# One visit of the array for the logits of two token groups, and one exponential for both, in a list-scheduled attention and gMLP kernel

## The chip, the cores and the metric

The kernel runs on one core of a Trainium2 chip. The metric is the device time of one execution in microseconds (us), as a median over runs. The engines are named as in the profile: PE (TensorE, matmuls), PEld (its weight loads), DVE (VectorE), ACT (ScalarE), POOL (GpSimd) and SP (SyncE, which here only issues transfers).

## The reference

Two branches share one normalised input and are added to it. Branch A is a local attention with 32 heads of 16: each token sees itself and seven earlier tokens, two apart. Branch B is a gated MLP whose gate is mixed over the tokens by a 2048 x 2048 matrix.

```python
xn = _layernorm(x)                                  # x: 2048 tokens x 512
# A
q, k, v = heads(xn @ wqkv)                          # 32 heads of 16
idx = pos[:, None] - 2 * arange(8)[None, :]         # masked where idx < 0
logits = einsum('bhsd,bhswd->bhsw', q, k[idx]) * 16 ** -0.5
A = einsum('bhsw,bhswd->bhsd', softmax(logits), v[idx]).reshape(B, S, D) @ wo
# B
z = _gelu(xn @ w_in); z1 = z[..., :896]; z2 = _layernorm(z[..., 896:])
g = einsum('ts,bsf->btf', w_sp, z2) + b_sp[None, :, None]
B = (z1 * g) @ w_out
out = x + A + B
```

## The kernel before, in words

The 2048 tokens are cut into 16 blocks of 128 and into 4 groups j of 512 (NJ = 4). Every step is recorded as a task with an engine, its inputs and outputs, a guessed duration and a priority. Then one list schedule (`Plan.schedule`, L123, called at L1004) walks through guessed time, picks for each engine the task that can start first (among those within `tol` ns of it, the one with the lowest priority number, L191), and gives each task that needs PSUM one of the 8 banks, or a pair of them. What comes out is a fixed order for each engine. On the chip each engine works through its order and waits on semaphores. The guessed rates and durations (`dma_bw`, `dma_lat`, `tol`, `est`) therefore change nothing but the orders and the choice of banks.

Steps that matter here, in rough order of time:

- Normalisation and transposes of x (to about 30 us); V of each block, `v_block` (L645), matmuls on L654, eviction by ACT on L663, a POOL-issued store to DRAM on L668 (tasks Vw0 to Vw15).
- `z2_block` (L752): the gate's input half, matmuls on L759, gelu and square on ACT (L767, L772). Four blocks at a time are normalised: small DVE steps L778 to L785, a power on POOL (L788, tasks zr0 to zr3), and four DVE scalings (L791).
- `qk_pair` (L671): Q and K of a group, matmuls on L677, one ACT eviction L686.
- `prods` (L690): for a group, four DVE products q*k over all 8 offsets (L698) and three DVE additions (L703), all 128x4096 in bf16. The sum lies in buffer `pb` 0 or 2 (`acc`, by the parity of j); buffer 1 holds the product that is to be added. Then PE sums over the four partitions that hold parts of one head: eight matmuls with a weight of only 32 columns (E32), each writing 32 of the 128 partitions of PSUM (L711, task red0 to red3). This is one **visit**; its result takes a pair of banks.
- `softmax` (L718): DVE takes the maximum out of PSUM (L726) and subtracts it, PSUM to SBUF (L728; smax and ssub), ACT computes exp in place on 128x1024 bf16 (L732, sexp), DVE sums, inverts and scales (L735 to L745), and SP issues a transpose of the weights (L747, attnT).
- `z1_group` (L798): the other half of the MLP, matmuls on L805, gelu on ACT (L811). exp and gelu come from different tables of ACT, so each change between them is a table load (shown as ACT_TABLE_LOAD).
- `g_group` (L883): the token mixing, 448 matmuls on L894, copied out by ACT (L902) and combined by DVE (L905, L908).
- `pv_block` (L911): per block, SP loads 8 shifted copies of V (L917, 1 MB each), DVE multiplies and adds (L922, L925, L928), SP transposes the result (L931).
- `out_block` (L936): both output projections into one bank (L950, L959), a DVE addition of x (L965), a store (L970).

SP has a single queue for nearly all transfers, and its order is part of the schedule too. Before the change, each group goes through `softmax(j, prods(j))` by itself (L851 to L854).

Of the kernel before, what the change touches and what calls it, by code (L numbers as in the profile page):

```python
# [11 lines left out]
ACTF = mybir.ActivationFunctionType  # L12
# [326 lines left out]
def build_kernel(nc, A_x, A_wqkv, A_wo, B_x, B_w_in, B_w_sp, B_b_sp, B_w_out, out, report=False, emit=True):  # L339
    S = A_x.shape[1]  # L340
    D = A_x.shape[2]
    assert D == 512 and S % 512 == 0
    NB = S // 128
    NJ = S // 512
# [14 lines left out]
    off = {}  # L359
# [34 lines left out]
    plan = Plan()  # L394

    with ExitStack() as es:
        ar = es.enter_context(nc.sbuf_tensor("arena", [128, AR], BF))
        fp = es.enter_context(nc.sbuf_tensor("fpool", [128, FR], F32))
        ps = es.enter_context(nc.psum_tensor("ps", [128, PR], F32))
        sem_h = {e: es.enter_context(nc.semaphore("sem_" + e)) for e in ENGS if e != "sp"}  # L400

        def A(name, n, o2_=0):
            return ar[:, off[name] + o2_: off[name] + o2_ + n]

        def AC(o_, dims):
            return bass.AP(tensor=ar, offset=o_, ap=[[AR, 128]] + [list(d) for d in dims])
# [73 lines left out]
        def c_act(n, psum=True, accum=False):  # L480
            return (170.0 if psum else 205.0) + n * 0.833 + (200.0 if accum else 0.0)
# [7 lines left out]
        T = plan.add  # L489

        def dma(eng, fn, nbytes, chan, reads=(), writes=(), name="", xbar=False, prio=0.0, after=()):
# [4 lines left out]
        E32 = A("E32", 32)  # L496
# [10 lines left out]
          writes=["ident"], est=300, name="ident1")  # L507
# [27 lines left out]
        def ld_wqk(which, eng):  # L535
# [6 lines left out]
            writes=[("xin0", 0), ("xin0", 1)], name="ldx0")  # L542
# [15 lines left out]
        for wi in range(NWARM):  # L558
            n_ = 512 if wi < 6 else 128
            T("pe", (lambda bw, n_: lambda t: t.matmul(P(bw, n_), ones[:, 0:128], ones[:, 0:n_], start=True,  # L560
                                                       stop=True))(bw, n_),
              writes=[bw], est=(427.0 if n_ == 512 else 107.0), name="warm%d" % wi, prio=1000)

        T("act", lambda a: a.activation(Fv("prime", 4), mhalf, ACTF.Gelu_apprx_tanh), reads=["mhalf"],
          writes=["prime"], est=1500, name="actprime", tbl="gelu")
# [105 lines left out]
        def qk_pair(j, c):  # L671
            bk = plan.bank("QK%d_%d" % (j, c), 2)
            for which in range(2):
                def mm(t, which=which):
                    last = None
                    for dc in range(4):
                        last = t.matmul(P(bk, 512, 512 * which),  # L677
                                        AC(off["wqk"] + 2048 * which + 512 * dc + c, [[4, 128]]),
                                        AC(off["xnT"] + dc * S + 512 * j, [[1, 512]]), start=(dc == 0),
                                        stop=(dc == 3))  # L680
                    return last
                T("pe", mm, reads=[("wqk", which)] + [("xnT", b) for b in range(4 * j, 4 * j + 4)], writes=[bk],
                  est=4 * c_mm(512), name="%s%d_%d" % ("QK"[which], j, c), prio=10 + 18 * j + c)
            qo = off["QT"] + 2048 * (j % 2) + 512 * c
            ko = off["KT"] + c * (S + KP) + KP + 512 * j
            T("act", lambda a: a.activation(AC(qo, [[ko - qo, 2], [1, 512]]),  # L686
                                            P(bk, 1024).rearrange("p (t n) -> p t n", t=2), ACTF.Copy, scale=0.5),
              reads=[bk], writes=[("QT", c, j % 2), ("KT", c, j)], est=c_act(1024), name="QKe%d_%d" % (j, c), prio=1)

        def prods(j):  # L690
            acc = (0, 2)[j % 2]
            for c in range(4):
                s_ = acc if c == 0 else 1
                qb = AC(off["QT"] + 2048 * (j % 2) + 512 * c, [[0, 8], [1, 512]])
                kb = AC(off["KT"] + c * (S + KP) + KP + 512 * j, [[-2, 8], [1, 512]])
                pbv = A("pb", 4096, 4096 * s_).rearrange("p (w s) -> p w s", w=8)
                rd = [("QT", c, j % 2), ("KT", c, j), ("KT", c, j - 1) if j > 0 else ("KTpad", c)]
                T("dve", (lambda pbv, qb, kb: lambda v: v.tensor_tensor(pbv, qb, kb, ALU.mult))(pbv, qb, kb),  # L698
                  reads=rd, writes=[("pb", s_)], est=c_tt(4096), name="prod%d_%d" % (j, c), prio=5 + j)
                if c > 0:  # L700
                    av = A("pb", 4096, 4096 * acc)
                    bv = A("pb", 4096, 4096 * 1)
                    T("dve", (lambda av, bv: lambda v: v.tensor_tensor(av, av, bv, ALU.add))(av, bv),  # L703
                      reads=[("pb", 1)], writes=[("pb", acc)], est=c_tt(4096), name="padd%d_%d" % (j, c), prio=5 + j)
            bk = plan.bank("lg%d" % j, 2)

            def mm(t):
                last = None
                for hf in range(2):
                    for a in range(4):  # L710
                        last = t.matmul(ps[32 * a:32 * a + 32, bk.col(512 * hf):bk.col(512 * hf) + 512], E32,  # L711
                                        AC(off["pb"] + 4096 * acc + 2048 * hf + 128 * a, [[512, 4], [1, 128]]),
                                        start=True, stop=True)
                return last
            T("pe", mm, reads=[("pb", acc), "E32"], writes=[bk], est=600.0, name="red%d" % j, prio=1)
            return bk

        def softmax(j, bk):  # L718
            ds = j % 2
            if j == 0:  # L720
                def msk(v):
                    lg = bass.AP(tensor=ps, offset=bk.col(), ap=[[PR, 32], [128, 8], [1, 16]])
                    return v.tensor_tensor(lg, lg, bass.AP(tensor=fp, offset=foff["maskt"],
                                                           ap=[[FR, 32], [16, 8], [1, 16]]), ALU.add)
                T("dve", msk, reads=["maskt"], writes=[bk], est=300, name="smask", prio=4)
            T("dve", lambda v: v.tensor_reduce(Fv("mx", 128), PC(bk.col(), [[1, 128], [128, 8]]), AX.X, ALU.max),  # L726
              reads=[bk], writes=["mx"], est=1218, name="smax%d" % j, prio=4)
            T("dve", lambda v: v.tensor_tensor(A("D", 1024, 1024 * ds).rearrange("p (w t) -> p w t", w=8),  # L728
                                               PC(bk.col(), [[128, 8], [1, 128]]),
                                               FCa(foff["mx"], [[0, 8], [1, 128]]), ALU.subtract),  # L730
              reads=[bk, "mx"], writes=[("D", ds)], est=1222, name="ssub%d" % j, prio=4)
            T("act", lambda a: a.activation(A("D", 1024, 1024 * ds), A("D", 1024, 1024 * ds), ACTF.Exp),  # L732
              writes=[("D", ds)], est=c_act(1024, psum=False), name="sexp%d" % j, tbl="exp", prio=(2, 7, 2, 2)[j], late=3)
            do = off["D"] + 1024 * ds
            T("dve", lambda v: v.tensor_tensor(A("Za", 512), A("D", 512, 1024 * ds), A("D", 512, 1024 * ds + 512),  # L735
                                               ALU.add),
              reads=[("D", ds)], writes=["Za"], est=c_tt(512), name="sz1_%d" % j, prio=4)
            T("dve", lambda v: v.tensor_tensor(Fv("Zb", 256), A("Za", 256), A("Za", 256, 256), ALU.add),
              reads=["Za"], writes=["Zb"], est=423, name="sz2_%d" % j, prio=4)
            T("dve", lambda v: v.tensor_tensor(Fv("Z", 128), Fv("Zb", 128), Fv("Zb", 128, 128), ALU.add),  # L740
              reads=["Zb"], writes=["Z"], est=292, name="sz3_%d" % j, prio=4)
            T("dve", lambda v: v.reciprocal(A("R", 128), Fv("Z", 128)), reads=["Z"], writes=["R"], est=952,
              name="srec%d" % j, prio=4)
            dv = A("D", 1024, 1024 * ds).rearrange("p (w t) -> p w t", w=8)
            T("dve", lambda v: v.tensor_tensor(dv, dv, AC(off["R"], [[0, 8], [1, 128]]), ALU.mult),  # L745
              reads=["R"], writes=[("D", ds)], est=c_tt(1024), name="sattn%d" % j, prio=4)
            dma("sp", lambda e: e.dma_start_transpose(AC(off["attn"] + 1024 * j, [[128, 8], [1, 128]]),  # L747
                                                      A("D", 1024, 1024 * ds)),
                128 * 1024 * 2, ("attnT", ds), reads=[("D", ds)], writes=[("attn", b) for b in range(4 * j, 4 * j + 4)],
                name="attnT%d" % j, xbar=True, prio=1)  # L750
# [66 lines left out]
        for b in range(8, NB):  # L817
# [10 lines left out]
          writes=[("KTpad", c) for c in range(4)], est=170, name="ktpad", prio=2, after=lnr[:8])  # L828
# [19 lines left out]
            512 * 896 * 2, "w_in1", writes=["w_in1"], name="ldwin1", prio=2, after=lnd[4:8])  # L848
        for j in range(NJ):
            z2_wave(j)  # L850
        for j in range(NJ):  # L851
            for c in range(4):
                qk_pair(j, c)
            softmax(j, prods(j))  # L854
        for j in range(NJ):
            for pr in PAIRS:
                z1_group(pr, j)
# [132 lines left out]
        for names in (["warm%d" % wi for wi in range(NWARM)] +  # L990
# [9 lines left out]
            for n0, n1 in zip(names, names[1:]):  # L1000
                if byname[n0] not in byname[n1].deps:
                    byname[n1].odeps.add(byname[n0])

        plan.schedule(tol=30.0, dma_bw=270.0, dma_lat=1300.0, overlap=40.0,  # L1004
                      land=dict(ldx0=3580.0, ldx1=4700.0, ldwv0=4050.0, ldwv1=5300.0, ldx2=5700.0, ldwin2a=6950.0, ldwin2b=8250.0,
                                ldx3=8650.0, ldx4=9050.0, ldx5=9400.0, ldx6=9750.0, ldx7=10200.0, ldq=11700.0, ldk=13200.0))
        if report:
# [49 lines left out]
```

## Time and profile before

| | |
|---|---|
| median of 3 runs | 238.06 us (237.9 to 238.14) |
| the profiled execution | 237.62 us |
| its span, first to last instruction | 236.2 us |
| granted TensorE clock | 1.000 |
| PE: matmuls | 1135 |
| matmuls of the token mixing (L894) | 97.0 us of PE's busy time |
| visits for the logits (L711) | 4, at 48.62, 71.62, 94.72 and 122.14 us |
| ACT: exp (L732) | 4 of 1055 ns, with 3 table loads |
| DVE: products and additions (L698, L703) | 28 of about 2.28 us |

The span is the time between the first and the last instruction of the program; the 1.4 us between it and the execution's time lie around the program. A matmul's busy time counts from its start to its modelled end, and the next one starts before that end. So the distance between the starts of two matmuls is what one of them costs, and not its duration. "x8" in a timeline stands for eight instructions of one kind that were merged into one row: the row has the start of the first and the time to the end of the last.

### The profile page before, as it was taken

To read this page: it belongs to the slowest core of one execution; us is meant where nothing else is said; L and a number is where in the kernel's file an instruction comes from. 1 tells how busy PE (TensorE), PEld (TensorE's weight loads), DVE (VectorE), ACT (ScalarE), POOL (GpSimd) and SP (SyncE) were. 2 spreads that over 40 slices of the span, in tenths; PEclk is the share of its full clock that TensorE was granted. 3 is DMA by queue.
4 is the path that set the end of the run, shared out by engine and by line. 5 is a ranking of instruction groups with operands and counts; after the bars stand their busy time and mean duration, and the time that the engine had idled before them with its cause. 6 is when DMAs were issued, how large, how long until landed. Compare 5 with 4: busy or idle time off the path is not lost.

```text
span 236.2 us, 2999 instructions
## 1 busy us (share of the span) xinstructions
PE 233.4 (99%) x1135; PEld 109.2 (46%) x1135; DVE 206.9 (88%) x269; ACT 98.8 (42%) x149; POOL 37.0 (16%) x56
## 2 busy tenths in 40 slices
PE   8999999999999999999999999999999999999996
PEld 3555555545444444444444444444444444444443
DVE  4799899999899999998899999844899998999732
ACT  3698989888979896631120311111111111000000
POOL 2268650312943400000000000000000000000000
DMA  6997969991058800430579999999666959944442
GB/s 205 362 286 192 205 152 218 172 217 42 3 191 284 166 31 20 148 77 10 193 241 322 214 217 253 242 230 326 205 207 206 276 176 248 290 131 156 111 134 69
DMA packets 82013, 43.86 MB, mean 186 GB/s; under 512 B 54336, under 2 KB 81360, under 8 KB 82000
## 3 DMA queue, kind: packets, MB, share of 16 engines
q1 hardware_dynamic: 80768, 41.27, 69.1%
q0 software_dynamic: 800, 2.11, 2.7%
q10 hardware_dynamic: 432, 0.30, 0.4%
q8 instruction: 9, 0.15, 0.2%
q14 instruction: 4, 0.03, 0.1%
HBM read 26.35 MB, written 4.21 MB: 129 GB/s over the span
## 4 chain that ended last, share of the span: by engine, by line
PE 99%; DVE 0%; issue 0%; DVEq 0%
PE ps L894 41%; PE ps L677 12%; PE ps L759 10%; PE ps L805 10%; PE ps L959 10%; PE ps L654 6%; PE ps L950 6%; PE ps L560 1%; PE ps L711 1%; PE ps L579 1%; PE ps L638 1%; DVE arena L965 0%; DVEq L319 0%
## 5 line engine op out<-in xcount | busy, mean ns | idle before, releaser
L894 PE MATMUL ps<-arena 128*128 128x512 bf16 x448 | 97.0, 379 | 0.0
L894 PEld LDWEIGHTS ps<-arena 128*128 128x128 bf16 x448 | 43.8, 98 | 53.0 <-issue 0.4
L902 ACT ACTIVATE arena<-ps 128x1024 bf16<-128x1024 f32 (+1 forms) x16 | 14.7, 917 | 78.8 <-PE ps L894 78.8
L922 DVE TENSOR_TENSOR arena<-arena 128x4096 bf16<-128x4096 bf16 x16 | 36.5, 2284 | 0.0
L698 DVE TENSOR_TENSOR arena<-arena 128x4096 bf16<-128x4096 bf16 x16 | 36.3, 2275 | 0.0
L925 DVE TENSOR_TENSOR arena<-arena 128x2048 bf16<-128x2048 bf16 (+1 forms) x32 | 30.3, 950 | 0.1
L677 PE MATMUL ps<-arena 128*128 128x512 bf16 x128 | 28.9, 379 | 0.0
L703 DVE TENSOR_TENSOR arena<-arena 128x4096 bf16<-128x4096 bf16 x12 | 27.4, 2282 | 0.0
L959 PE MATMUL ps<-arena 128*128 128x512 bf16 (+2 forms) x119 | 27.0, 366 | 0.0
L759 PE MATMUL ps<-arena 128*128 128x448 bf16 x128 | 26.0, 353 | 0.0
L805 PE MATMUL ps<-arena 128*128 128x512 bf16 x112 | 24.5, 379 | 0.0
L677 PEld LDWEIGHTS ps<-arena 128*128 128x128 bf16 x128 | 14.5, 114 | 13.0
L905 DVE TENSOR_TENSOR arena<-arena 128x1024 bf16<-128x1024 bf16 (+1 forms) x16 | 10.0, 623 | 11.2 <-ACT arena L902 11.1
L965 DVE TENSOR_TENSOR arena<-ps,arena 128x512 bf16<-128x512 f32 (+2 forms) x17 | 11.2, 657 | 9.0 <-PE ps L959 8.8
L759 PEld LDWEIGHTS ps<-arena 128*128 128x128 bf16 x128 | 12.4, 98 | 11.9 <-issue 0.4
L686 ACT ACTIVATE arena<-ps 128x1024 bf16<-128x1024 f32 x16 | 16.3, 1018 | 3.4 <-PE ps L677 2.2
L959 PEld LDWEIGHTS ps<-arena 128*128 128x128 bf16 x119 | 11.4, 98 | 12.8
L788 POOL TENSOR_TENSOR fpool<-fpool 128x4 f32<-128x4 f32 x4 | 14.3, 3583 | 18.0 <-DVE fpool L785 18.0
L805 PEld LDWEIGHTS ps<-arena 128*128 128x128 bf16 x112 | 10.9, 98 | 13.4 <-issue 0.4
L950 PE MATMUL ps<-arena 128*128 128x512 bf16 (+2 forms) x68 | 16.6, 366 | 0.0
L654 PE MATMUL ps<-arena 128*128 128x512 bf16 x64 | 16.6, 387 | 0.0
L811 ACT ACTIVATE arena<-ps 128x1024 bf16<-128x1024 f32 (+1 forms) x16 | 14.0, 920 | 5.3 <-PE ps L805 5.3
(62 smaller groups left out, 181.8 us busy)
## 6 DMA issues: line engine op xcount, KB each, us to landing
arena<-vscr SPq DMA_DIRECT2D x16, 1024.0 KB, 5.8
arena<-in_A_x_dram SPq DMA_DIRECT2D x30, 128.0 KB, 4.0
vscr<-arena POOLq DMA_DIRECT2D x16, 128.0 KB, 3.1
out_dram<-arena SPq DMA_DIRECT2D x15, 128.0 KB, 1.9
arena<-in_A_wqkv_dram SPq DMA_DIRECT2D x2, 512.0 KB, 6.1
arena<-in_B_w_in_dram SPq DMA_DIRECT2D x2, 448.0 KB, 5.4
arena<-in_B_w_in_dram SPq DMA_DIRECT2D x1, 896.0 KB, 5.6
arena<-in_B_w_out_dram SPq DMA_DIRECT2D x1, 896.0 KB, 5.3
```

Of the source, the lines that this page charges most:

```text
L654: last = t.matmul(P(bk, 512), A("xcT", 128, 512 * b + 128 * dc) if b < 2 else xTv(b, dc), A("wv", 512, 512 * dc), start=(dc == 0), stop=(d ...
L677: last = t.matmul(P(bk, 512, 512 * which), AC(off["wqk"] + 2048 * which + 512 * dc + c, [[4, 128]]), AC(off["xnT"] + dc * S + 512 * j, [[1 ...
L686: T("act", lambda a: a.activation(AC(qo, [[ko - qo, 2], [1, 512]]), P(bk, 1024).rearrange("p (t n) -> p t n", t=2), ACTF.Copy, scale=0.5), ...
L698: T("dve", (lambda pbv, qb, kb: lambda v: v.tensor_tensor(pbv, qb, kb, ALU.mult))(pbv, qb, kb), reads=rd, writes=[("pb", s_)], est=c_tt(40 ...
L703: T("dve", (lambda av, bv: lambda v: v.tensor_tensor(av, av, bv, ALU.add))(av, bv), reads=[("pb", 1)], writes=[("pb", acc)], est=c_tt(4096 ...
L759: last = t.matmul(P(bk, 448, 512 * hf), xTv(b, dc), AC(off["w_in2"] + 896 * dc + 448 * hf, [[1, 448]]), start=(dc == 0), stop=(dc == 3))
L805: last = t.matmul(P(bk, 512, 512 * i), AC(off["w_in1"] + 896 * dc + 128 * fc, [[1, 128]]), AC(off["xnT"] + dc * S + 512 * j, [[1, 512]]), ...
L894: last = t.matmul(P(bk, 512, 512 * i), AC(off["z2"] + FH * sh + 128 * fc, [[1, 128]]), AC(off["wT%d" % r_] + sh * 512, [[1, 512]]), start= ...
L922: T("dve", lambda v: v.tensor_tensor(tv, tv, av, ALU.mult), reads=[("attn", b)], writes=[("Vs", sv)], est=c_tt(4096), name="pv%d" % b, pri ...
L925: T("dve", (lambda n: lambda v: v.tensor_tensor(A("Vs", n, 4096 * sv), A("Vs", n, 4096 * sv), A("Vs", n, 4096 * sv + n), ALU.add))(n), wri ...
L950: last = t.matmul(P(bk, cn), AC(off["OT"] + 512 * tb + 128 * cc, [[1, 128]]), AC(off["wo"] + 512 * cc + c0, [[1, cn]]), start=(cc == 0), s ...
L959: last = t.matmul(P(bk, cn), AC(off["z1T"] + fc * S + 128 * tb, [[1, 128]]), AC(off["w_out"] + 512 * fc + c0, [[1, cn]]), start=False, sto ...
```

## The change

The matmuls of two groups' logits become one task, which waits for both groups' sums and writes two pairs of banks. The maximum and the subtraction stay one per group, and one exponential over 128x2048 then does both groups. The loop takes the groups in pairs: (0, 1) and (2, 3). The schedule is called with other guesses. No other task is added or taken away.

```diff
-            bk = plan.bank("lg%d" % j, 2)
+        def logits(j0):
+            bks = [plan.bank("lg%d" % j, 2) for j in (j0, j0 + 1)]
 
             def mm(t):
                 last = None
-                for hf in range(2):
-                    for a in range(4):
-                        last = t.matmul(ps[32 * a:32 * a + 32, bk.col(512 * hf):bk.col(512 * hf) + 512], E32,
-                                        AC(off["pb"] + 4096 * acc + 2048 * hf + 128 * a, [[512, 4], [1, 128]]),
-                                        start=True, stop=True)
+                for bk, acc in zip(bks, (0, 2)):
+                    for hf in range(2):
+                        for a in range(4):
+                            last = t.matmul(...)
                 return last
-            T("pe", mm, reads=[("pb", acc), "E32"], writes=[bk], est=600.0, name="red%d" % j, prio=1)
-            return bk
-
-        def softmax(j, bk):
+            T("pe", mm, reads=[("pb", 0), ("pb", 2), "E32"], writes=bks, est=1050.0, name="red%d" % j0, prio=1)
+            return bks
+
+        def smax(j, bk):
...
-            T("act", lambda a: a.activation(A("D", 1024, 1024 * ds), A("D", 1024, 1024 * ds), ACTF.Exp),
-              writes=[("D", ds)], est=c_act(1024, psum=False), name="sexp%d" % j, tbl="exp", prio=(2, 7, 2, 2)[j], late=3)
+
+        def sexp(j0):
+            T("act", lambda a: a.activation(A("D", 2048), A("D", 2048), ACTF.Exp),
+              writes=[("D", 0), ("D", 1)], est=c_act(2048, psum=False), name="sexp%d" % j0, tbl="exp", prio=2, late=3)
+
+        def softmax(j):
...
-        for j in range(NJ):
-            for c in range(4):
-                qk_pair(j, c)
-            softmax(j, prods(j))
+        for j0 in range(0, NJ, 2):
+            for j in (j0, j0 + 1):
+                for c in range(4):
+                    qk_pair(j, c)
+                prods(j)
+            for j, bk in enumerate(logits(j0), j0):
+                smax(j, bk)
+            sexp(j0)
+            for j in (j0, j0 + 1):
+                softmax(j)
...
-        plan.schedule(tol=30.0, dma_bw=270.0, dma_lat=1300.0, overlap=40.0,
+        plan.schedule(tol=50.0, dma_bw=300.0, dma_lat=1600.0, overlap=40.0,
```

The orders that come out differ from about 25 us on. The pair's visits are red0 (groups 0 and 1) and red2 (groups 2 and 3). In the new order of PE red0 stands among the last V blocks, and red2 behind 88 matmuls of the token mixing; before, red3 stood behind 108 of them. ACT has one table load before each of the two exponentials and one back to gelu behind the first.

More of the change, by code (lines that the diff above doesn't have):

```diff
@@ L704, in prods @@
                       reads=[("pb", 1)], writes=[("pb", acc)], est=c_tt(4096), name="padd%d_%d" % (j, c), prio=5 + j)
-            bk = plan.bank("lg%d" % j, 2)
+        def logits(j0):
+            bks = [plan.bank("lg%d" % j, 2) for j in (j0, j0 + 1)]
             def mm(t):
                 last = None
-                for hf in range(2):
-                    for a in range(4):
-                        last = t.matmul(ps[32 * a:32 * a + 32, bk.col(512 * hf):bk.col(512 * hf) + 512], E32,
-                                        AC(off["pb"] + 4096 * acc + 2048 * hf + 128 * a, [[512, 4], [1, 128]]),
-                                        start=True, stop=True)
-                return last
-            T("pe", mm, reads=[("pb", acc), "E32"], writes=[bk], est=600.0, name="red%d" % j, prio=1)
-            return bk
-        def softmax(j, bk):
+                for bk, acc in zip(bks, (0, 2)):
+                    for hf in range(2):
+                        for a in range(4):
+                            last = t.matmul(ps[32 * a:32 * a + 32, bk.col(512 * hf):bk.col(512 * hf) + 512], E32,
+                                            AC(off["pb"] + 4096 * acc + 2048 * hf + 128 * a, [[512, 4], [1, 128]]),
+                                            start=True, stop=True)
+                return last
+            T("pe", mm, reads=[("pb", 0), ("pb", 2), "E32"], writes=bks, est=1050.0, name="red%d" % j0, prio=1)
+            return bks
+        def smax(j, bk):
             ds = j % 2
@@ L731, in softmax @@
               reads=[bk, "mx"], writes=[("D", ds)], est=1222, name="ssub%d" % j, prio=4)
-            T("act", lambda a: a.activation(A("D", 1024, 1024 * ds), A("D", 1024, 1024 * ds), ACTF.Exp),
-              writes=[("D", ds)], est=c_act(1024, psum=False), name="sexp%d" % j, tbl="exp", prio=(2, 7, 2, 2)[j], late=3)
+        def sexp(j0):
+            T("act", lambda a: a.activation(A("D", 2048), A("D", 2048), ACTF.Exp),
+              writes=[("D", 0), ("D", 1)], est=c_act(2048, psum=False), name="sexp%d" % j0, tbl="exp", prio=2, late=3)
+        def softmax(j):
+            ds = j % 2
             do = off["D"] + 1024 * ds
```

## The prediction

> **What bounds the kernel now.** I read the page's busy times and its chain first, then PE's waits, then the timeline around one visit for the logits, on PE and on PEld. The page:
>
> ```profile
> PE 233.4 (99%) x1135; PEld 109.2 (46%) x1135; DVE 206.9 (88%) x269; ACT 98.8 (42%) x149; POOL 37.0 (16%) x56
> ...
> PE 99%; DVE 0%; issue 0%; DVEq 0%
> ```
>
> The chain that ended last is PE from beginning to end. PE's waits:
>
> ```profile
> engine line waited for: us in total, times, longest us
> PE ps L560 <- PEq L1042: 0.8, 1, 0.8
> ```
>
> The only wait of PE that counts is at the program's start. So DVE, ACT, POOL and transfers cost nothing as long as they deliver in time, and a step saves time only if it takes time out of PE's own stream. What the stream loses shows around the fourth visit (start, duration, then the group):
>
> ```profile
> 121.40 0.81 PE L894 MATMUL ps<-arena 128*128 128x512 bf16 x3
> 122.14 0.61 PE L711 MATMUL ps<-arena 128*32 128x512 bf16 x8
> 122.69 1.04 PE L894 MATMUL ps<-arena 128*128 128x512 bf16 x4
> ```
>
> and on PEld in the same window:
>
> ```profile
> 122.14 0.12 PEld L711 LDWEIGHTS ps<-arena 128*32 128x32 bf16 x8 [0.42 <-DVE arena L905]
> 122.68 0.76 PEld L894 LDWEIGHTS ps<-arena 128*128 128x128 bf16 x5 [0.42 <-issue]
> ```
>
> A dense 512-column matmul takes 0.2157 us from start to start (108 of L894 lie between 98.73 and 122.14, with the entry into the visit among them; 96 of L805 between 73.91 and 94.72). Three from 121.40 would let the next start at 122.05; the visit starts at 122.14, so **entering costs 0.09**. In the visit the eight matmuls run four at a time. It lasts 0.61, one matmul of it 0.38, so the second four start 0.23 after the first. The next ordinary matmul starts 0.55 after the visit's start, 0.32 after the second four: **leaving costs 0.10** over a dense step. The two idle times of 0.42 on PEld are these stops: no weight is loaded ahead across the border. The other three visits have the same distances (48.62 to 49.17, 71.62 to 72.17, 94.72 to 95.27), so none of them waited for data.
>
> **The change, part by part.**
>
> 1. *Four visits of 8 become two of 16.* One visit of 8 costs 0.09 + 0.23 + 0.32 = 0.64. One of 16 costs 0.09 + 3 x 0.23 + 0.32 = 1.10, against 1.28 for two. Saved: 0.19 a pair, **0.38 in all**, all of it on PE's path. Not shown before: a third and a fourth four in one visit. From below nothing is saved, if the change to the other pair of banks stops the array as an ordinary border does (though the second four already go to another bank, and start 0.23 later); from above each of the four borders that go is worth a matmul's whole tail, 0.379 - 0.216 = 0.16, 0.65 in all. I take 0.38, the measured borders.
>
> 2. *red0 now waits for group 1's sums, and stands later in PE's order.* By PE's rows up to 63.98, plus four V matmuls (0.86), less the earlier visit (0.64), plus the entry, it starts at 64.3. On DVE the last addition of group 1 ended at 71.02. Ten instructions that stood ahead of it now stand behind it: a product, smask, smax0, ssub0, four scalings of L791, two small sums, 7.0 us with 0.08 of overlap each taken off; and the idle 0.94 ahead of L791. It ends near 63.1. Spare 1.2; cost nothing.
>
> 3. *red2 stands 88 matmuls into the token mixing, and DVE's last addition of group 3 stands right behind a step that waits for that mixing* (gb2_0, L905). From the 64th matmul on: tail 0.16 and handover 0.04, ACT copy 1.02, DVE addition 0.69 less 0.08, last addition 2.28, together 4.1. PE has 24 matmuls in that time, 5.2. Spare 1.1; cost nothing. This holds whatever DVE did earlier, as it waits there: it stood 0.6 idle at this step before, and now has 5.2 us less softmax work ahead of the addition.
>
> 4. *Both pairs of banks are held until the subtractions are done.* PE's z1 group 2 takes over lg0's banks at about 75.4. DVE after 63.1: a product to 65.4, then four scalings that wait for POOL's power zr2. That is queued behind one V store more than before (Vw6), and zr2's own input is ready at 60.8; with the longest power in the rows it ends at 66.1. Scalings, smask, a product, smax0, an addition, ssub0 follow: 74.8. Spare 0.6. Banks of lg1 are taken at 79.7, and ssub1 ends at 77.3.
>
> 5. *One exponential of 2048.* This is the tightest place. The ACT rows of one exponential between two gelus:
>
> ```profile
> 80.82 1.28 ACT L732 ACT_TABLE_LOAD   x1
> 82.11 1.06 ACT L732 ACTIVATE arena<-arena 128x1024 bf16<-128x1024 bf16 x1
> 83.19 1.28 ACT L811 ACT_TABLE_LOAD   x1
> 84.48 3.83 ACT L811 ACTIVATE arena<-ps 128x1024 bf16<-128x1024 f32 x5
> ```
>
> and from the answers for single lines (duration ns min/median/max):
>
> ```profile
> L732 ACT ACTIVATE arena<-arena x4: 1049/1056/1057, 61.2 to 131.6; 128x1024 bf16<-128x1024 bf16 x4
> L811 ACT ACTIVATE arena<-ps x16: 592/1024/1032, 76.6 to 99.0; 128x1024 bf16<-128x1024 f32 x12, 128x512 bf16<-128x512 f32 x4
> L788 POOL TENSOR_TENSOR fpool<-fpool x4: 3014/3051/5217, 31.9 to 79.8; 128x4 f32<-128x4 f32 x4
> ```
>
> From the two forms of L811 512 elements more cost 0.43, so 2048 cost 1.056 + 0.86 = 1.92 (at least 1.06, at most twice 1.056 = 2.11). In the new order the exponential stands between gelu z1g2_0 and gelu z1g4_0, and PE's task z1_4_1 waits for z1g4_0's banks. From the first matmul of z1_3_0: its four end after 3 x 0.216 + 0.38 = 1.03, handover 0.04, gelu 1.02, load and start 1.31, exp 1.92, load 1.31, gelu 1.02: banks free at 7.65. PE has nine tasks of four matmuls until z1_4_1: 7.77. Spare 0.12. What a released PE needs is bounded by 4.1 to 5.0 us: the first of two L606 rows (382 ns from 4.23) ends at 4.61, the weight load that it released starts at 4.66 and takes 0.10: 0.05 to 0.15. So the cost is **0 to 0.03**, 0.22 with the longest exp. I take 0. ACT's saved table loads (5 after the first become 3) are worth nothing: it idles 78.8 us ahead of L902 alone.
>
> 6. *The new order of transfers.* attnT0 moves on SP from 75 to about 89 us; nothing needed sooner stands behind it. wT2 waits for the last visit and comes about 4 us earlier than its 124.5; its last part landed at 140.46, and PE uses it at 147.7. Later softmax for groups 2 and 3 delays their attention weights, but group 3's left at 156.1 before and its V blocks end the DVE work: the last transpose landed at 224.98 for a use at 231.69. Spare 7 us on both; nothing.
>
> *Sum:* 237.62 - 0.38 = 237.24 for the profiled execution, span 235.8. It lies 0.44 under the median of the runs, so for the median: 238.06 - 0.38 = **237.7**, 0.16% less.
>
> **Rivals.**
>
> - *The softmax pair comes late (slower).* If POOL's power zr2 pays for each V store queued ahead of it (5.22 against 3.05, 1.25 us behind one store: 2.17 a store; two stores 7.4), the scalings start 2.15 later, ssub0 frees its banks at 77.0 and PE stands still for 1.6: 238.06 - 0.38 + 1.6 = **239.3**. It decides from a power longer than 5.8. For it: DVE already idled 0.94 for this power. Against it: the second store is 2.6 us older than the first and should be done.
> - *The exponential blocks PE.* With 2.11 for exp and 0.15 to release PE: 237.9. A stronger form: each of the two table loads is followed by an idle time as long as itself, 2 x 1.28, and PE stands 2.5 us: 240.2 (slower). The rows above speak against it, 0.01 from the end of a load to the next instruction. The Trainium skill (ScalarE: Activation LUTs, What ACT_TABLE_LOAD costs) has this rule: about 1.38 us of drain beside a load of 1.28. The load agrees with the rows, the drain doesn't show in them.
> - *It doesn't save what it says.* The 16 matmuls stop between the two groups as at a border: 238.06.
>
> **How the numbers follow.** Forecast 0.67, at 237.7; exp of 2.11 0.10, at 237.9; nothing saved 0.08, at 238.1; late softmax 0.10, at 239.3; idle after table loads 0.02, at 240.2; a transfer late against all the spare above 0.03, slower. What a measurement of this kernel can tell from no change is about 0.2%, 0.48 us; the forecast lies below that. The three runs spread over 0.24, so of the forecast's 0.67 I give 0.18 to a result beyond 0.48. Faster 0.18; same 0.49 + 0.10 + 0.08 = 0.67; slower 0.15. Range: from 237.3 (0.65 saved, less half the spread) to 238.3 (nothing saved and the longest exp), about 0.82 of the chances.
>
> **What would show it.** Right: PE's list of waits stays with one row; two L711 groups of 16, about 1.07 long (three times 0.23 and 0.38), near 64 and 117 us; the next ordinary matmul 1.00 after their start. Part 5 wrong: idle PE time ahead of L812, released by ACT, near 84 us. Part 4 wrong: idle time of PE near 75 us behind DVE, and an L795 row over 5.8 us. Part 1 wrong: L711's successor (L713) starts over 1.1 us after the visit. Wrong as a whole if PE waits anywhere after 10 us.

## The result, and the profile after

The changed kernel takes 237.24 us (median of 6 runs, 237.05 to 237.31), the kernel before 237.98 in the 6 runs beside them (237.69 to 238.17). The ratio is 0.9972, with a 95% interval of 0.9962 to 0.9982. So the change saves 0.74 us by the medians and 0.67 by the ratio, where 0.38 was forecast. The time lies within 0.5 us of the forecast, but on the other side of the 0.2% that was named as the bound of no change: the forecast gave this 0.18 of its chances, for scatter alone. As a time, 237.24 lies 0.06 below the range that it named (237.3 to 238.3); with the ratio, 238.06 x 0.9972 = 237.39, it lies just inside.

The profiled execution of the changed kernel took 237.29 us, its span 236.1. Line numbers are now those of the changed kernel: L713 was L711 before (the visits), L766 was L759, L812 was L805, L907 was L894, L818 was L811, L736 was L732, L795 was L788, L728 and L730 were L726 and L728. First the page's busy times and its chain:

```profile
PE 231.7 (98%) x1114; PEld 109.1 (46%) x1135; DVE 207.4 (88%) x269; ACT 96.5 (41%) x145; POOL 32.7 (14%) x56
...
PE 94%; DMA 3%; SPq 1%; ACT 1%; issue 1%; DVE 0%
```

Two readings here would mislead. PE's 231.7 stands beside 233.4 before, but 21 records of matmuls are missing in this trace: x1114 beside 1135 weight loads. A difference of busy times is no measure of what was saved. And the chain is no longer PE alone. PE's waits say why:

```profile
engine line waited for: us in total, times, longest us
PE ps L560 <- PEq L1055: 0.8, 1, 0.8
PE ps L766 <- DMA arena<-in_B_w_in_dram: 0.5, 2, 0.3
```

The second row is new. In the timeline of PE (start, duration, group) it lies at the very beginning:

```profile
7.34 0.59 PE L654 MATMUL ps<-arena 128*128 128x512 bf16 x2
8.22 0.92 PE L766 MATMUL ps<-arena 128*128 128x448 bf16 x4 [0.28 <-DMA arena<-in_B_w_in_dram]
9.34 0.93 PE L766 MATMUL ps<-arena 128*128 128x448 bf16 x4 [0.21 <-DMA arena<-in_B_w_in_dram]
```

PE waits there for the two loads of the gate's half of `w_in`, long before 25 us, where the orders of the two kernels begin to differ. A second profile of the same kernel (after_again, below) has no such wait in PE's list. So an effect of the first microseconds of one execution lies on top of the change, and span against span (236.2 to 236.1) doesn't give the worth of the change. I therefore cut each profiled execution at two events of PE that every kernel has: the start of the first Q matmul (the first L677) and the start of the last matmul. **Head** is the time up to the first, **body** the time between them, **tail** what follows to the end of the span, and **outside** the execution's time less its span.

| us | head | body | tail | outside |
|---|---|---|---|---|
| before | 14.95 | 219.09 | 2.12 | 1.46 |
| after | 15.31 | 218.65 | 2.10 | 1.23 |

The body became 0.44 shorter and the time outside the span 0.23 shorter. The head became 0.36 longer in these two executions. That the profiled execution came so close to its forecast (237.29 for 237.24) is therefore luck: the longer head took back what was saved outside the span and what the visits saved beyond the forecast. The two visits, on PE:

```profile
63.69 1.03 PE L654 MATMUL ps<-arena 128*128 128x512 bf16 x4
64.64 1.05 PE L713 MATMUL ps<-arena 128*32 128x512 bf16 x16
65.62 0.60 PE L654 MATMUL ps<-arena 128*128 128x512 bf16 x2
...
98.23 19.16 PE L907 MATMUL ps<-arena 128*128 128x512 bf16 x86
117.31 1.05 PE L713 MATMUL ps<-arena 128*32 128x512 bf16 x16
118.29 77.87 PE L907 MATMUL ps<-arena 128*128 128x512 bf16 x353
```

A visit of 16 lasts 1.05, and the next ordinary matmul starts 0.98 after it. A visit of 8 was 0.55 from its start to the same point.

### The profile page after: what moved, and what is told of

It is laid out like the page before. It is cut to its first block, busy times and chain, and to the rows that moved or that the text cites. A ratio compares the mean times of both kernels' runs of the same rounds, so it can differ in the third digit from the quotient of the medians.

```text
span 236.1 us, 2974 instructions
## 1 busy us (share of the span) xinstructions
PE 231.7 (98%) x1114; PEld 109.1 (46%) x1135; DVE 207.4 (88%) x269; ACT 96.5 (41%) x145; POOL 32.7 (14%) x56
## 4 chain that ended last, share of the span: by engine, by line
PE 94%; DMA 3%; SPq 1%; ACT 1%; issue 1%; DVE 0%
PE ps L907 41%; PE ps L677 12%; PE ps L972 10%; PE ps L812 10%; PE ps L766 9%; PE ps L963 6%; PE ps L654 5%; DMA arena<-in_B_w_in_dram 3%; PE ps L713 1%; ACT arena L774 0%; SPq L518 0%; ACT arena L587 0%; PE ps L579 0%; SPq L514 0%; SPq L524 0%
## 5 line engine op out<-in xcount | busy, mean ns | idle before, releaser
L907 PE MATMUL ps<-arena 128*128 128x512 bf16 x439 | 96.6, 379 | 0.5
L907 PEld LDWEIGHTS ps<-arena 128*128 128x128 bf16 x448 | 43.7, 98 | 53.1 <-issue 0.4
L677 PE MATMUL ps<-arena 128*128 128x512 bf16 x126 | 28.7, 379 | 0.1
L766 PE MATMUL ps<-arena 128*128 128x448 bf16 x128 | 26.0, 352 | 0.5 <-DMA arena<-in_B_w_in_dram 0.5
L812 PE MATMUL ps<-arena 128*128 128x512 bf16 x110 | 24.4, 379 | 0.1
L677 PEld LDWEIGHTS ps<-arena 128*128 128x128 bf16 x128 | 14.5, 113 | 13.0
L766 PEld LDWEIGHTS ps<-arena 128*128 128x128 bf16 x128 | 12.3, 98 | 12.7 <-ACT arena L642 0.7
L812 PEld LDWEIGHTS ps<-arena 128*128 128x128 bf16 x112 | 10.9, 98 | 13.2 <-ACT arena L818 0.3
L774 ACT ACTIVATE arena<-ps 128x896 bf16<-128x896 f32 x16 | 14.6, 914 | 3.2 <-PE ps L766 3.1
L818 ACT ACTIVATE arena<-ps 128x1024 bf16<-128x1024 f32 (+1 forms) x16 | 13.9, 923 | 4.9 <-PE ps L812 4.8
L654 PE MATMUL ps<-arena 128*128 128x512 bf16 x60 | 15.6, 379 | 0.2
L779 ACT ACTIVATE arena<-arena 128x896 bf16<-128x896 bf16 x16 | 15.1, 945 | 0.0
```

The source lines that it names most:

```text
L654: last = t.matmul(P(bk, 512), A("xcT", 128, 512 * b + 128 * dc) if b < 2 else xTv(b, dc), A("wv", 512, 512 * dc), start=(dc == 0), stop=(d ...
L677: last = t.matmul(P(bk, 512, 512 * which), AC(off["wqk"] + 2048 * which + 512 * dc + c, [[4, 128]]), AC(off["xnT"] + dc * S + 512 * j, [[1 ...
L766: last = t.matmul(P(bk, 448, 512 * hf), xTv(b, dc), AC(off["w_in2"] + 896 * dc + 448 * hf, [[1, 448]]), start=(dc == 0), stop=(dc == 3))
L812: last = t.matmul(P(bk, 512, 512 * i), AC(off["w_in1"] + 896 * dc + 128 * fc, [[1, 128]]), AC(off["xnT"] + dc * S + 512 * j, [[1, 512]]), ...
L907: last = t.matmul(P(bk, 512, 512 * i), AC(off["z2"] + FH * sh + 128 * fc, [[1, 128]]), AC(off["wT%d" % r_] + sh * 512, [[1, 512]]), start= ...
```

## The experiments

The code lines below are shortened to what an edit changes. Ten kernels ran, in three groups beside the kernel before, which took 237.69 us (32 runs), 237.85 (25) and 237.93 (19) there. Their bodies, heads and times outside the span are in one table; the texts below take them from it. "Outside, mean" is over all runs of the kernel (its time less its span), and the last column counts all instructions of DVE in the trace, its waits on semaphores and its register instructions included.

| us | head | body | outside, profiled | outside, mean (runs) | DVE |
|---|---|---|---|---|---|
| before | 14.95 | 219.09 | 1.46 | 1.467 (32), 1.460 (25), 1.453 (19) | 310 |
| after | 15.31 | 218.65 | 1.23 | 1.25 (6) | 309 |
| after_again | 14.37 | 218.65 | 1.23 | 1.243 (9) | 309 |
| visits_4 | 14.91 | 219.09 | 1.23 | 1.226 (12) | 309 |
| visits_8 | 14.90 | 220.01 | 1.23 | 1.238 (12) | 309 |
| sched_only | 15.13 | 219.09 | 1.54 | 1.488 (12) | 310 |
| sp_pad | 14.63 | 218.65 | 1.23 | 1.255 (10) | 309 |
| dve_pad | 14.81 | 218.65 | 1.45 | 1.487 (10) | 310 |
| exp_8 | 15.29 | 219.24 | 1.23 | 1.256 (10) | 309 |
| visit_only | 14.95 | 218.65 | 1.32 | 1.278 (4) | 308 |
| before_less | 15.45 | 219.09 | 1.24 | 1.249 (10) | 309 |
| dve_pad4 | 15.00 | 218.65 | 1.63 | 1.616 (10) | 312 |

### The changed kernel once more

No edit.

> The changed kernel once more, unchanged. Theory V (only the two visits that went save time, 0.207 us each by the trace of after: 0.094 to enter and 0.98 from the visit's start to the next ordinary matmul, against two times 0.094 + 0.547): 0.41 us under the kernel before, ratio 0.9983. Rival S (the new orders, or something else that came with them, give another 0.33): 0.74 under it, ratio 0.9969.

It took 236.96 us in 9 runs, a ratio of 0.9961 (0.9945 to 0.9978). That is 0.73 less by the medians, near the 0.74 of rival S and not the 0.41 of theory V: something beside the visits saves time. It is not in the body, which is the same as in the first profile to 0.01. The head is 0.94 shorter, and PE's list of waits has one row again. The stretch that showed the two waits:

```profile
7.11 0.59 PE L654 MATMUL ps<-arena 128*128 128x512 bf16 x2
7.54 1.79 PE L766 MATMUL ps<-arena 128*128 128x448 bf16 x8
```

The eight matmuls of L766 follow one another with only 0.11 us lost (1.79, where the next eight take 1.68). So the size of the wait for `w_in` belongs to an execution and not to the kernel, and the head scatters by nearly 1 us between executions.

The loads are not the whole of it. The longest head, 15.45 in before_less (below), has no wait for a load in PE's list. There the first matmuls run slowly for longer. The first pair of L654, in after_again and then in before_less:

```profile
4.63 0.60 PE L654 MATMUL ps<-arena 128*128 128x512 bf16 x2
```

```profile
4.99 1.06 PE L654 MATMUL ps<-arena 128*128 128x512 bf16 x2
```

A single matmul of 512 columns takes 0.63 us in the slow stretch and 0.38 later. The slow stretch is over by 4.1 us in after_again and lasts to 6.7 in before_less, so the second pair of L654 starts at 5.72 in the one and at 7.00 in the other. Why its length differs was not tested. The body doesn't scatter: it is the place to read the change.

### The visit cut in two and in four

The changed kernel, with its orders kept. The 16 matmuls become two tasks of 8 (visits_4) or four of 4 (visits_8), and one ordinary task of PE is put between any two of them:

```diff
+t.eng, t.fn, t.est, t.name, t.dma, t.tbl = "pe", fn, 100.0, "%s_%d" % (red.name, k), None, None
...
+plan.order["pe"].insert(at + 2 * k, t)
```

The mask, maximum and subtraction of the first group wait for the first half alone, those of the second group for the last part.

> The changed kernel with its orders kept, but each visit of 16 matmuls cut into two of 8 with one ordinary PE task between them: four visits as before the change. Theory V: the saving is gone, the same time as the kernel before (ratio 1.000). Rival S: 0.33 us under the kernel before remain (ratio 0.9986). In the trace both give four visits with 0.09 at the entry and about 0.55 from start to the next ordinary matmul.

> The same with each visit of 16 cut into four of 4: eight visits. Theory V: six visits more than in the changed kernel, 6 x 0.207 = 1.24 us over it and 0.83 over the kernel before (ratio 1.0035). Rival S: also 1.24 over the changed kernel, but 0.5 over the kernel before (1.0021). If a border costs less when the visits lie close together, the step from four to eight visits is below 0.83.

visits_4 took 237.42 us (0.9990, 0.9973 to 1.0007), visits_8 238.33 (1.0026, 1.0013 to 1.0039). These times can't decide between V and S: visits_4's interval holds both forecasts, and visits_8 lies between them. The bodies can. With two visits more the body is again that of the kernel before, 219.09; with four more on top it is 220.01, 0.92 longer, 0.23 a visit. PE in visits_8, where the visits are on L716:

```profile
63.28 1.03 PE L654 MATMUL ps<-arena 128*128 128x512 bf16 x4
64.23 0.40 PE L716 MATMUL ps<-arena 128*32 128x512 bf16 x4
64.56 0.60 PE L654 MATMUL ps<-arena 128*128 128x512 bf16 x2
65.10 0.40 PE L716 MATMUL ps<-arena 128*32 128x512 bf16 x4
65.43 0.60 PE L654 MATMUL ps<-arena 128*128 128x512 bf16 x2
```

From one visit's start to the next one's is 0.87, for four small matmuls and two ordinary ones. Dense, these are three steps of 0.216, together 0.65: a visit costs 0.22 in borders, one way in and one way out. The number of visits alone accounts for the whole difference of the bodies. What visits_4 still seems to save against before (0.27 by the medians, in an interval that includes no saving) is not in its body; the time outside is shorter, 1.23 against 1.47. So V is right for the body, and of the 0.33 that rival S added, 0.24 lies outside the span.

### One part alone

sched_only is the kernel before with the planner's new guesses, visit_only the changed kernel with the old ones:

```diff
-plan.schedule(tol=30.0, dma_bw=270.0, dma_lat=1300.0, overlap=40.0,
+plan.schedule(tol=50.0, dma_bw=300.0, dma_lat=1600.0, overlap=40.0,
```

> The kernel before with only the schedule's figures of the change (tol 50, transfers 300 per ns and 1600 ns): other orders, four visits and four exponentials. Theory V: no difference, ratio 1.000, PE without waits after the start. Rival S: 0.33 us under the kernel before, ratio 0.9986.

> The changed kernel with the schedule's figures of the kernel before (tol 30, 270 per ns, 1300 ns). SP has 135 instructions, DVE 308, ACT 145. If only the visits count, first Q to last matmul is 218.65 as in the changed kernel; if the figures are part of the gain, it is longer. Outside the span: theory SP 1.47 or more, theories DVE and ACT 1.24.

sched_only took 237.79 us (0.9998, 0.9984 to 1.0013), with the body of the kernel before. visit_only took 236.78 us (4 runs; 0.9952, 0.9936 to 0.9967), with the body of the changed kernel. The planner's guesses are worth nothing in the body either way; all 0.44 come from the merged visits. visit_only's lead over the changed kernel is not in the body either, and lies within the scatter of the heads.

### One instruction more on SP or on DVE

The time outside the span fell by 0.22 to 0.24 in the changed kernel, in visits_4 and in visits_8, and not in sched_only. It lies outside what the profile shows, so I looked for what these kernels have in common. Counted over their traces, DVE has 309 instructions for 310 (one wait on a semaphore fewer), SP 133 for 134 and ACT 145 for 148 (without its 32 reads of an accumulator). sp_pad gives SP one more at its end (the two waits are one instruction in the trace), dve_pad gives DVE one more at its start, in the changed kernel:

```diff
+for c in sorted(out_chans)[:2]:                       # sp_pad
+    eng.wait_ge(chan_sems[c], plan.chan_totals[c])
...
-v.memset(zeros, 0.0)                                  # dve_pad
+[v.memset(A("zeros", 256, 256 * i), 0.0) for i in range(2)][-1]
```

> The changed kernel with one more instruction on SP: at the very end it waits once more for two transfers that have landed. In the runs so far the execution's time exceeds its span by 1.47 us in the kernel before and in sched_only, and by 1.24 in the four kernels with the paired exponential. The streams of SP, DVE and ACT are all shorter in these (SP 133 against 134 instructions, DVE 309 against 310, ACT 145 against 148). Theory SP (the length of SP's stream decides): 1.47 outside the span here. Theories ACT and DVE: 1.24. Time from the first Q matmul to the last matmul: 218.65 in all of them.

> The changed kernel with one more instruction on DVE: the first memset is done in two halves (DVE idles there until x lands). Theory DVE: 1.47 outside the span; theories SP and ACT: 1.24. First Q matmul to last matmul: 218.65.

With SP's instruction the time outside stayed at 1.255, with DVE's it went back to 1.487, that of the kernel before. The medians can't show this (237.43 and 237.32, ratios 0.9984 with 0.9969 to 0.9999, and 0.9984 with 0.9966 to 1.0001): the heads of both scatter by more. ACT's count is ruled out by exp_8 below, where ACT has 159 instructions, counted the same way, and 1.256 us lie outside. visit_only has more SP instructions than any (135) and 1.278 outside, which speaks against SP once more.

### The kernel before with one instruction less on DVE, and the changed one with three more

If DVE's count is what matters, the kernel before must gain without any part of the change. before_less gives the clearing of a small buffer at the start to POOL; dve_pad4 cuts it into four on DVE in the changed kernel:

```diff
-T("dve", lambda v: v.memset(zeros, 0.0), writes=["zeros"], est=200, name="zeros")
+T("pool", lambda v: v.memset(zeros, 0.0), writes=["zeros"], est=200, name="zeros")
```

> The kernel before with its first memset moved from DVE to POOL: DVE has 309 instructions in place of 310, SP (134) and ACT (148) as in the kernel before; the other orders are the same. If the length of DVE's stream decides the time outside the span: 1.24 in place of 1.47, and first Q to last matmul 219.09 as before. If something else of the kernel before does (the single exponentials, their table loads): 1.47.

> The changed kernel with its first memset in four quarters: DVE has 312 instructions. If there is a step in DVE's length between 309 and 310: 1.47 outside the span, as with 310 (dve_pad, 1.49). If it goes by some alignment of the stream's end, it may be 1.24 again. First Q to last matmul 218.65.

before_less has 1.249 us outside, against 1.453 for the kernel before in the same group, and takes 237.59 (0.9986, 0.9975 to 0.9997), with an unchanged body. dve_pad4 has 1.616, neither of the two values that were expected. So the time outside follows the length of DVE's stream in both kernels: 1.28 us at 308 instructions, 1.25 at 309, 1.46 to 1.49 at 310, 1.62 at 312. It isn't a straight line, and the runs don't show what happens in this time.

The trace of dve_pad4 misses no matmul, and its page shows what the busy times of the changed kernel hid:

```profile
PE 233.0 (99%) x1135; PEld 109.3 (46%) x1135; DVE 207.4 (88%) x272; ACT 96.6 (41%) x145; POOL 32.7 (14%) x56
```

PE is busy for 233.0 us, against 233.4 before with the same 1135 matmuls; the slow matmuls of the head are in both sums.

The spans of all runs can now be set against the bodies. Their mean is 235.92 us for dve_pad4 beside 236.38 for the kernel before in its group, 235.92 for dve_pad beside 236.35, and 235.68 for after_again beside 236.21: 0.43 to 0.53 less, as the 0.44 of the body says, so the change doesn't move the head. sp_pad, with the same body, is the exception (236.25 beside 236.35); its runs lie between 235.5 and 237.3, and what made them longer is open.

### The exponential made longer

This tests the spare that was reckoned for the tightest place. In the changed kernel the exponential is cut into eight of 256:

```diff
-a.activation(A("D", 2048), A("D", 2048), ACTF.Exp)
+[a.activation(A("D", 256, 256 * i), A("D", 256, 256 * i), ACTF.Exp) for i in range(8)][-1]
```

> The changed kernel with each exponential of 2048 issued as eight of 256, in the same place of the same orders; 14 instructions more on ACT. By the exp rows (1056 ns for 1024, 1910 for 2048) one of 256 takes 0.42, and eight with 0.10 of overlap each 2.63: 0.72 longer. If the place after the first exponential is as tight as counted (spare 0 to 0.05), PE waits 0.65 to 0.75 for z1_4_1's banks near 84.5 us, and first Q to last matmul is 219.3 to 219.4. If there is hidden spare, it stays at 218.65. Outside the span: theory ACT (length of ACT's stream) says more than 1.24, SP and DVE say 1.24.

It took 237.67 us (0.9995, 0.9986 to 1.0004). The body grew by 0.59, to 219.24, a little less than expected. ACT and PE in that stretch:

```profile
78.72 1.28 ACT L736 ACT_TABLE_LOAD   x1
80.02 2.56 ACT L736 ACTIVATE arena<-arena 128x256 bf16<-128x256 bf16 x8
82.60 1.28 ACT L818 ACT_TABLE_LOAD   x1
```

```profile
83.31 1.24 PE L812 MATMUL ps<-arena 128*128 128x512 bf16 x5
84.97 2.33 PE L812 MATMUL ps<-arena 128*128 128x512 bf16 x10 [0.42 <-ACT arena L818]
```

The exponentials take 2.56, 0.65 more than the one of 1.91, and PE's task z1_4_1 now waits for ACT, at the place that the prediction named. Its idle time shows as 0.42 and not as 0.59, because idle time counts from the modelled end of the matmul before, 0.16 after a dense next start. Of 0.65, 0.59 reach the end: the spare in the changed kernel is 0.06.

## Why the prediction was right or wrong

**What bounds the kernel: right.** After 10 us PE waits for nothing, and what the two merged visits save by their rows is found again in the body, to 0.01 us. "PE's list of waits stays with one row" failed in one profile and held in the other: the second row came from the loads of `w_in`, before 10 us.

**Step 1, the visits: the mechanism right, the size too small.** Forecast 0.38, measured 0.44. The merged visit doesn't stop between the two groups. The third and fourth four follow at the dense 0.216, not at the 0.23 by which the second follows the first. I took this 0.23 for the step of fours as such. The printed terms give 0.18 a pair (1.28 less 1.10); the 0.19 that was used is the two borders, 0.09 and 0.10, added. With 0.094 for the way in, 0.547 from a visit's start to the next ordinary matmul, and 0.01 by which that matmul's own step is longer (0.226), two visits of 8 cost 2 x 0.651 = 1.302. One of 16 costs 0.094 + 0.98 + 0.01 = 1.084. That is 0.22 a pair, 0.44 for two: of the 0.04 beyond 0.18, 0.03 are the third and fourth steps and 0.01 the longer step behind the visit. The Trainium skill (TensorEngine Tiling (Array Packing), Key Properties) says that a change of tiling mode drains the array, without a figure. This agrees with the rows: here a way in and out costs 0.22.

**Steps 2 and 3, the waits for the sums: right.** The last additions of groups 1 and 3, on DVE:

```profile
60.90 2.29 DVE L703 TENSOR_TENSOR arena<-arena 128x4096 bf16<-128x4096 bf16 x1
```

```profile
113.91 2.28 DVE L703 TENSOR_TENSOR arena<-arena 128x4096 bf16<-128x4096 bf16 x1
```

The first ended at 63.19 (forecast 63.1). The visits started at 64.64 and 117.31, and PE's list has no wait ahead of them. The forecast 64.3 was for a head of the length before; this one was 0.36 longer. The addition of group 3 ended at 116.19, 1.1 ahead of its visit, as reckoned.

**Step 4, the banks: right.** POOL's power zr2 isn't slowed by the second V store ahead of it, and the subtraction came earlier than reckoned. The answer for the power's line, and rows from the timelines of POOL and DVE:

```profile
L795 POOL TENSOR_TENSOR fpool<-fpool x4: 1041/3050/3057, 32.2 to 76.6; 128x4 f32<-128x4 f32 x4
```

```profile
61.02 3.06 POOL L795 TENSOR_TENSOR fpool<-fpool 128x4 f32<-128x4 f32 x1 [0.62 <-DVE fpool L792]
```

```profile
72.98 1.21 DVE L730 TENSOR_TENSOR arena<-ps,fpool 128x1024 bf16<-128x1024 f32 x1
```

zr2, at 61.02, is the longest power, 3.06, where 5.22 was allowed for; the subtraction ends at 74.19 instead of 74.8. The rival of a late softmax pair, which needed a power over 5.8, falls. Why zr2 took 5.22 before stays open.

**Step 5, the exponential: right, by little.** ACT's timeline:

```profile
77.71 1.02 ACT L818 ACTIVATE arena<-ps 128x1024 bf16<-128x1024 f32 x1 [0.70 <-PE ps L812]
78.75 1.28 ACT L736 ACT_TABLE_LOAD   x1
80.04 1.91 ACT L736 ACTIVATE arena<-arena 128x2048 bf16<-128x2048 bf16 x1
81.97 1.28 ACT L818 ACT_TABLE_LOAD   x1
83.27 5.83 ACT L818 ACTIVATE arena<-ps 128x1024 bf16<-128x1024 f32 x7
```

The exponential takes 1.91 (forecast 1.92), and both loads are followed by the next instruction 0.01 to 0.02 later: no idle time after a table load, so that rival falls too. On PEld, z1_4_1 shows how near it was:

```profile
84.34 0.61 PEld L812 LDWEIGHTS ps<-arena 128*128 128x128 bf16 x4 [0.26 <-ACT arena L818]
```

The weight load had to wait 0.26 for the banks, but no matmul was late: PE's list has no such wait. The spare was put at 0.12 less 0.05 to 0.15 for releasing PE; exp_8 shows 0.06 left.

**Step 6, the transfers: right in what it cost.** No matmul after 10 us waits for one in the changed kernel. The single arrival times that it named are not shown here.

**The sum: this is the step that failed.** It set the span's saving against the profiled execution and kept the 1.4 us around the span as a constant, without a reason. It was not constant: 0.22 was saved there, because DVE's stream became one instruction shorter. Of the 0.74 between the medians, 0.44 are the visits and 0.22 lie outside the span. The remaining 0.08 is no more than the scatter of the heads; by the ratio, 0.67, nothing remains. That the outside time depends on DVE's count was shown on both kernels (before_less, dve_pad, dve_pad4); why it does, and why not in a straight line, stays open.

## What to carry to other kernels

When one engine runs without a gap, count each step on it from start to start, and count the switches between forms of work: here a short visit of another matmul shape costs 0.22 us whatever its length, so merging visits pays as long as the steps behind them keep their spare. To measure tenths of a microsecond, compare the time between two fixed events of the bounding engine, since the execution's time also holds how its first microseconds went and what lies outside the span. Before merging two short steps of another engine into a long one, work out the next release behind it: here it had 0.06 us left.

## What the runs showed of the hardware

- The time between an execution and its span, 1.23 to 1.63 us in these profiles, changes with the number of DVE instructions: 0.2 us between 309 and 310.
- The time to the first Q matmul scattered between 14.37 and 15.45 us over these profiles, by waits for `w_in` (up to 0.5 us) and by how long the first matmuls of 512 columns took 0.63 us each instead of 0.38; the 219 us of dense matmuls behind it repeated to 0.01 us for the same visits.
